# The recurrence pieces' work is queued behind the product of the preceding feed-forward block

## The chip, the cores and the metric

The kernel runs on one core of a Trainium2 chip. A core has TensorE (PE: matrix products, whose weight loads, PEld, run beside them), VectorE (DVE), ScalarE (ACT), GpSimd (POOL) and SyncE (SP), which here issues nearly all DMAs. Each engine takes its instructions in the order of its own queue and waits where an input isn't there or a buffer isn't free. The metric is the device time of one execution in microseconds: 883.58 us before, the median of 3 runs (882.69 to 884.54).

## What is computed

An mLSTM recurrence (4 batches, 8 heads, 768 tokens, head size 40) gives a [3072, 320] activation, and two gated feed-forward blocks follow, all in float32:

```
m' = max(f + m, i);  C = exp(f + m - m')*C + exp(i - m')*v k^T;  n likewise with k
y  = sigmoid(o) * (C q) / max(|n.q|, 1)                        # recurrence
x2 = (sigmoid(x @ w_gate) * (x @ w_val)) @ w_out               # block 1, d_ff 1536
out = (h * clip(h + 3, 0, 6) / 6) @ w_out2,  h = x2 @ w_in     # block 2, d_ff 2048
```

## The kernel before

The tokens are cut into 6 chunks of 128 tokens per batch, 512 columns for the matrix products. Float32 operands are split into a high and a low part, so that a product is three matmuls. A first stage, up to about 480 us, does the recurrence and block 1, interleaved; a second stage does block 2. The change touches the first stage alone.

Its loop (L858) runs over steps i = (chunk c, hidden block f, columns ts). A step is `m1_h` (L575): two groups of eight matmuls into the PSUM banks `mm` (three banks), the gate on ScalarE (L580, a sigmoid of the first bank), the product on VectorE (L581, gate times the second bank), and `split_g`, the high part on ScalarE (L567, gh) and the low part on VectorE (L568, gl). `m1_out` then multiplies gh and gl of an earlier step into `acc`. Most steps are 512 columns wide; the first 8 steps of chunk 0 and the first 12 of chunk 1 are 256 wide. Steps are counted from 0 here; step 44 is the 45th run of the loop.

The recurrence of chunk c, batch b, a set (c, b), is cut in three pieces, and as a rule one piece is issued per step, ahead of the step's `m1_h` (L863 to L871), about a chunk before block 1 needs its result:

- `att0` (L412): scores on TensorE (L363) into the two `att` banks; on VectorE two scans that turn a tile of decay factors, `dec`, into decays (L389), the values times the input gate and the decay (L354, vi and vd; for chunk 1 eight ScalarE scalings L352 make vi), and two products L404 that weigh the scores and free the two `att` banks; on ScalarE a small copy L383.
- `att1` (L426): output matmuls (L444, L455, L470, the last into a third `mm` bank), then on VectorE the chain L487, L490, L492 to L496, L354, L504 (for two sets of chunk 1 ScalarE does the scaling, eight L352), and the state update L522 and L525, which frees the `mm` bank; on ScalarE the output gate L410 and the state copies L530.
- `att2` (L532): three transposes on TensorE (L536) into an `att` bank, and the split of x on ScalarE (L541) and VectorE (L542), which frees the bank.

`dec` has two buffers. The load of the set two ahead is issued when `att1` of a set is issued (L873 to L877) and waits on SyncE for the buffer. In between `work` (L656) prepares weights: L101 (ScalarE), L119, L122 (VectorE) unpack one, L151 to L174 split one for block 1, and L632 (four times), L634 and L635 combine one for block 2.

The order of each engine's queue is not the order of the code. A list scheduler builds the queues from the traced instructions by its own costs. `tc.issue_after(ins)` sets an edge from `ins` to each instruction of its block on the same engine, so that none of them comes ahead of `ins` in the queue; on other engines it does nothing. Before, `later_chunks`, the pieces of chunk 0 and the weight work have such edges; the pieces of chunks 1 to 5 have none (L869: `opened if cp == 0 else ()`).

Of the kernel before, what the change touches and what calls it, by code (L numbers as in the profile page):

```python
# [14 lines left out]
ALU = mybir.AluOpType  # L15
# [17 lines left out]
def mlstm_then_two_gated_ffn(  # L33
# [11 lines left out]
    nc = tc.nc  # L45
# [12 lines left out]
    def ps_mm():  # L58
        return mm_ps.tile([P, 512], F32, tag="mm", name="mm")
# [132 lines left out]
    def x_tiles(key):  # L192
        x = xpool.tile([P, 2, 3, T], F32R, tag="x", name="x")
        XH[key], XL[key] = x[:, 0], x[:, 1]
# [5 lines left out]
    def att_tiles(c, b):  # L200
        if c == 0 and b > 1:
            t = slot_f32(2 * NP * L).rearrange("p (a n l) -> p a n l", a=2, l=L)
            v = slot_f32(3 * DM).rearrange("p (a n) -> p a n", a=3)
            d = slot_f32(H * L).rearrange("p (h l) -> p h l", l=L)
        else:
            t = ap.tile([P, 2, NP, L], F32, tag="qk", name="qk")
            v = ap.tile([P, 3, DM], F32, tag="vko", name="vko")
            d = ap.tile([P, H, L], F32, tag="dec", name="dec")
        at[c, b] = {"qk": t, "vko": v, "dec": d}

    def qk_load(c, b):
        nc.sync.dma_start(out=at[c, b]["qk"], in_=qkT[c, b])

    def vko_load(c, b):
        nc.sync.dma_start(out=at[c, b]["vko"], in_=vko[c, b])

    def att_load(c, b):
        att_tiles(c, b)
        qk_load(c, b)
        vko_load(c, b)  # L220

    def dec_load(c, b):
        nc.sync.dma_start(
            out=at[c, b]["dec"].rearrange("p h l -> p (h l)"),
            in_=fz_dram[c, b * H : (b + 1) * H, :]
            .rearrange("h l -> (h l)")
            .rearrange("(o n) -> o n", o=1)
            .to_broadcast([P, H * L]),
        )
# [4 lines left out]
    g = g_sb[:, :S].rearrange("p (c l) -> p c l", l=L)  # L234
# [56 lines left out]
    def later_chunks():  # L291
# [43 lines left out]
        out=sel, in_=ident[:BH, :BH].rearrange("p (n two) -> p n two", two=2),  # L335
# [4 lines left out]
        out=odd[:, :, 0], in_=ident[:BH, :BH].rearrange("p (n two) -> p two n", two=2),  # L340
# [4 lines left out]
        out=par.rearrange("p (two n) -> p two n", two=2), in_=odd.to_broadcast([BH, 2, 64])  # L345
# [186 lines left out]
    def att2(c, b, ps):  # L532
        yo = at.pop((c, b))["yo"]
        x_ps = ps()
        for k in range(3):
            nc.tensor.transpose(  # L536
                out=x_ps[:, k * P : (k + 1) * P], in_=yo[:, k * P : (k + 1) * P], identity=ident
            )
        x_v = x_ps[:, : 3 * P].rearrange("p (k t) -> p k t", k=3)
        xs = slice(b * L, (b + 1) * L)  # L540
        hi = nc.scalar.copy(out=XH[1, c][:, :, xs], in_=x_v)  # L541
        lo = nc.vector.tensor_tensor(  # L542
            out=XL[1, c][:, :, xs], in0=x_v, in1=XH[1, c].bitcast(F32)[:, :, xs], op=ALU.subtract
        )
        return hi.ins, lo.ins

    def h_pair(w, x, banks, ts=slice(0, T)):

        xh, xl = XH[x][:, :, ts], XL[x][:, :, ts]
        for j in range(2):  # L550


            tail = w[:, j, 256:384]
            nc.tensor.matmul(out=banks[j], lhsT=tail, rhs=xl[:, 2, :], start=True, stop=False)  # L554
            for k in range(2):
                hi = w[:, j, k * P : (k + 1) * P]
                lo = w[:, j, 384 + k * P : 384 + (k + 1) * P]
                nc.tensor.matmul(out=banks[j], lhsT=hi, rhs=xh[:, k, :], start=False, stop=False)  # L558
                nc.tensor.matmul(out=banks[j], lhsT=hi, rhs=xl[:, k, :], start=False, stop=False)  # L559
                nc.tensor.matmul(out=banks[j], lhsT=lo, rhs=xh[:, k, :], start=False, stop=False)  # L560
            nc.tensor.matmul(out=banks[j], lhsT=tail, rhs=xh[:, 2, :], start=False, stop=True)  # L561

    def split_g(g):
        n = g.shape[-1]
        gh = gpool.tile([P, T], F32R, tag="gh", name="gh", bufs=3)[:, :n]
        gl = gpool.tile([P, T], F32R, tag="gl", name="gl", bufs=3)[:, :n]
        nc.scalar.copy(out=gh, in_=g)  # L567
        nc.vector.tensor_tensor(out=gl, in0=g, in1=gh.bitcast(F32), op=ALU.subtract)  # L568
        return gh, gl
# [5 lines left out]
    def m1_h(c, f, ts):  # L575
        n = ts.stop - ts.start
        banks = [ps_mm()[:, :n], ps_mm()[:, :n]]
        h_pair(slots["in", f], (1, c), banks, ts)
        g = gpool.tile([P, T], F32, tag="g", name="g")[:, :n]
        gate = nc.scalar.activation(out=g, in_=banks[0], func=AF.Sigmoid).ins  # L580
        nc.vector.tensor_tensor(out=g, in0=g, in1=banks[1], op=ALU.mult)  # L581
        gs[c, f, ts.start] = split_g(g)
        return gate

    def m1_out(c, f, ts):
        if f == 0 and ts.start == 0:
# [69 lines left out]
    def work(count, limit):  # L656

        for _ in range(count):
            if len(jobs) > n_jobs - limit:
                src, use, key = jobs.pop()  # L660
                use(key, to_f32(fetched.pop(0) if fetched else fetch(src)))

    def load_out2(n):
        x = xpool.tile([P, 640], F32, tag="x2", name="w2f")
        nc.sync.dma_start(out=x, in_=wo2_dram[n])
        split_out2(("out2", n), x)
# [27 lines left out]
    with tc.manual_schedule():  # L694
# [52 lines left out]
        for b in range(2):  # L747
            opened = att2(0, b, any_ps)
# [38 lines left out]
    def x_load(pair):  # L787


        b = {}  # L790
        for k in range(2):
            for j in range(2):
                src = x2_dram[2 * pair + j]
                t = b[k, j] = late.tile([P, 640], F32, tag="c", name="xr", bufs=7)
                nc.sync.dma_start(out=t[:, 0:T], in_=src[:, k, :])
                u = late.tile([P, 2, P], F32, tag="xt", name="xu", bufs=3)
                tails = src[:, 2, :].rearrange("(two k r) (q t) -> k q r two t", two=2, k=2, q=4)[k]
                for q in range(4):
                    nc.sync.dma_start(out=u[32 * q : 32 * q + 32], in_=tails[q])
                nc.vector.tensor_tensor(out=t[:, T:], in0=u[:, 0], in1=u[:, 1], op=ALU.add)  # L800
        return x_combine(pair, b)
# [49 lines left out]
    def outputs_but(n):  # L851
        while len(before) > n:
            step = before.pop(0)
            m1_out(*step)
            if step[1] == F1 - 1:
                m1_end(step[0])

    for i, (c, f, ts) in enumerate(steps):  # L858
        if i == halves[0] - 1:
            for b in range(2):  # L860
                att_load(1, b)
                dec_load(1, b)
        for _ in range(quota[i]):  # L863
            if pieces:
                cp, b, piece = pieces.pop(0)
                if cp > 0 and b == 0 and piece == 0:
                    x_tiles((1, cp))
                with ExitStack() as queued:
                    for ins in opened if cp == 0 else ():  # L869
                        queued.enter_context(tc.issue_after(ins))  # L870
                    (att0, att1, att2)[piece](cp, b, ps_att)  # L871
                nxt = divmod(cp * B + b + 2, B)
                if cp > 0 and piece == 1 and nxt[0] < NC:  # L873
                    att_tiles(*nxt)
                    dec_load(*nxt)
                    qk_load(*nxt)
                    vko_load(*nxt)  # L877
        gate = m1_h(c, f, ts)
        outputs_but(2 if i < n_two else 1)
        before.append((c, f, ts))  # L880
        if c == 0:
            work(1 if i < 2 * halves[0] else 2, n_w1)
        elif c < NC - 1:

            with tc.issue_after(gate):
                work(c > 1 and f % 2 == 0, n_jobs)
        elif f == 0:
            assert not jobs and not pieces
            early_sb.close()
            late = ctx.enter_context(tc.tile_pool(name="late", bufs=1, reuse_waits="tile"))  # L890
            x_parts = x_load(0)
            load_group(0)
        else:
            if f > 1 and f - 2 < F2 // 2:
                load_out2(f - 2)
            next(x_parts, None)
# [187 lines left out]
```

## Time and profile before

| | |
|---|---|
| median of 3 runs | 883.58 us (882.69 to 884.54) |
| profiled execution | 884.24 us, span 882.4 us |
| mean granted TensorE clock | 0.986 of full speed |
| busy over the span | PE 842.0 us (95%), DVE 568.2 (64%), ACT 397.7 (45%) |
| chain that ended last | PE 78%, DVE 12%, DMA 7% (all of it the load of `dec`) |

Busy shares are means over stages with different limits, so they are read by stretches. The idle time of an instruction is put down to what ended it: "[2.77 <-DVE x L542]" says that the engine stood for 2.77 us before this instruction, and that L542 on VectorE released it. A granted clock of 0.50 is TensorE at 1.2 in place of 2.4 GHz. In the order of a queue the scan L389 is listed as SCALAR_TENSOR_TENSOR, in the trace as TENSOR_TENSOR_SCAN.

### The profile page before, as it was taken

What the parts mean: (1) busy time and instruction counts of PE and PEld (TensorE: products, weight loads), DVE (VectorE), ACT (ScalarE), POOL (GpSimd) and SP (SyncE); (2) the same over time, 40 slices, a digit from 0 to 9 for tenths busy, and PEclk for the clock granted to TensorE, in tenths of its full rate; (3) what the DMA queues carried; (4) which work ended last, traced back from release to release, by engine and by line L of the source; (5) the groups of instructions that cost most, each with busy time, mean ns of one, the idle gap of its engine ahead of it and who ended that gap; (6) DMA issues with size and microseconds to landing.
All of it is one profiled execution on the core that took longest, in us unless ns stands there. A gap on an engine that the chain in (4) does not pass through costs nothing.

```text
span 882.4 us, 17342 instructions
## 1 busy us (share of the span) xinstructions
PE 842.0 (95%) x7109; PEld 719.2 (82%) x7109; DVE 568.2 (64%) x1040; ACT 397.7 (45%) x807; POOL 2.5 (0%) x8
## 2 busy tenths in 40 slices
PE   6599899999999899999899999999999999999998
PEld 6498688888777777777678888888998889988898
DVE  8899965675577657765754553566846668466553
ACT  3687633322323343333322443555645556365552
POOL 1000000000000000000000000000000000000000
PEclk9999999999999999999999999999999999999999
DMA  9636623332555645564541652546635467344400
GB/s 357 231 116 230 222 71 107 116 97 71 169 174 179 207 138 208 178 207 131 180 119 54 183 138 75 180 146 198 208 97 188 145 199 216 102 157 146 145 30 30
DMA packets 69135, 135.64 MB, mean 154 GB/s; under 512 B 20672, under 2 KB 43136, under 8 KB 65984
## 3 DMA queue, kind: packets, MB, share of 16 engines
q1 hardware_dynamic: 69008, 134.44, 47.3%
q8 instruction: 56, 0.92, 0.4%
q14 instruction: 23, 0.19, 0.1%
q10 hardware_dynamic: 48, 0.10, 0.0%
HBM read 109.38 MB, written 25.13 MB: 152 GB/s over the span
## 4 chain that ended last, share of the span: by engine, by line
PE 78%; DVE 12%; DMA 7%; issue 2%; ACT 1%; SPq 0%; DVEq 0%; ACTq 0%
PE mm L910 9%; PE acc L596 8%; DMA dec<-fz_dram 7%; PE mm L558 6%; PE mm L559 6%; PE mm L560 6%; PE att L910 5%; PE acc L910 4%; PE mm L554 4%; DVE dec L389 3%; PE mm L561 3%; PE acc L606 3%; PE mm L947 2%; PE acc L947 2%; PE mm L948 2%; PE mm L949 2%
## 5 line engine op out<-in xcount | busy, mean ns | idle before, releaser
L567 ACT CAST gh<-g 128x512 fp32r<-128x512 f32 (+1 forms) x130 | 76.4, 588 | 160.4 <-DVE g L581 120.3
L558 PE MATMUL mm<-x,w 128*128 128x512 f32 (+1 forms) x328 | 123.5, 376 | 0.0
L559 PE MATMUL mm<-x,w 128*128 128x512 f32 (+1 forms) x328 | 123.1, 375 | 0.0
L560 PE MATMUL mm<-x,w 128*128 128x512 f32 (+1 forms) x328 | 122.4, 373 | 0.0
L568 DVE TENSOR_TENSOR gl<-g,gh 128x512 fp32r<-128x512 f32 (+1 forms) x130 | 84.2, 647 | 57.2 <-ACT gh L567 56.8
L596 PE MATMUL acc<-gh,w 128*128 128x512 f32 (+1 forms) x328 | 104.9, 365 | 0.0
L910 PE MATMUL mm<-X,wg 128*128 128x512 f32 x336 | 85.3, 395 | 0.0
L389 DVE TENSOR_TENSOR_SCAN dec<-dec,ident 128x512 f32<-128x512 f32 x40 | 48.0, 1216 | 53.9 <-DMA dec<-fz_dram 53.9
L581 DVE TENSOR_TENSOR g<-g,mm 128x512 f32<-128x512 f32 (+1 forms) x82 | 50.5, 616 | 47.1 <-PE mm L561 46.8
L580 ACT ACTIVATE g<-mm 128x512 f32<-128x512 f32 (+1 forms) x82 | 44.7, 545 | 76.7 <-PE mm L561 76.4
L559 PEld LDWEIGHTS mm<-x,w 128*128 128x128 f32 x328 | 64.3, 196 | 11.2
L560 PEld LDWEIGHTS mm<-x,w 128*128 128x128 f32 x328 | 64.2, 196 | 11.3
L910 PEld LDWEIGHTS mm<-X,wg 128*128 128x128 f32 x336 | 62.0, 188 | 13.5 <-DVE c L921 0.3
L558 PEld LDWEIGHTS mm<-x,w 128*128 128x128 f32 x328 | 64.5, 197 | 9.0
L554 PE MATMUL mm<-x,w 128*128 128x512 f32 (+1 forms) x164 | 68.5, 418 | 3.3 <-DVE cst L525 2.9
L596 PEld LDWEIGHTS acc<-gh,w 128*128 128x128 f32 x328 | 60.8, 190 | 10.6
L561 PE MATMUL mm<-x,w 128*128 128x512 f32 (+1 forms) x164 | 60.7, 370 | 0.0
L596 PE MATMUL acc<-gl,w 128*128 128x512 f32 (+1 forms) x164 | 60.0, 366 | 0.0
L925 ACT ACTIVATE gb<-c,half 128x512 f32<-128x512 f32 x48 | 34.5, 724 | 49.0 <-DVE c L921 49.0
L568 DVE TENSOR_TENSOR gl<-gb,gh 128x512 fp32r<-128x512 f32 x48 | 33.1, 690 | 32.3 <-ACT gh L567 32.3
L910 PE MATMUL att<-X,wg 128*128 128x512 f32 x168 | 46.8, 398 | 0.1
L567 ACT CAST gh<-gb 128x512 fp32r<-128x512 f32 x48 | 29.5, 621 | 37.9 <-PE att L948 37.9
(185 smaller groups left out, 1695.6 us busy)
## 6 DMA issues: line engine op xcount, KB each, us to landing
wg<-ws_dram SPq DMA_DIRECT2D x24, 1104.0 KB, 5.6
raw<-in_w SPq DMA_DIRECT2D x20, 640.0 KB, 5.1
qk<-in_qkT SPq DMA_DIRECT2D x22, 512.0 KB, 4.5
wg<-wt_dram SPq DMA_DIRECT2D x48, 224.0 KB, 6.2
vko<-in_vko SPq DMA_DIRECT2D x22, 480.0 KB, 6.6
dec<-fz_dram SPq DMA_DIRECT2D x20, 512.0 KB, 5.1
raw<-in_wo SPq DMA_DIRECT2D x14, 640.0 KB, 3.9
X<-xt_dram SPq DMA_DIRECT2D x84, 64.0 KB, 3.1
```

The costliest lines, as they stand in the source:

```text
L389: nc.vector.tensor_tensor_scan(out=x, data0=a["factors"][n] if "factors" in a else x, data1=ident4.rearrange("p h l -> p (h l)"), initial= ...
L554: nc.tensor.matmul(out=banks[j], lhsT=tail, rhs=xl[:, 2, :], start=True, stop=False)
L558: nc.tensor.matmul(out=banks[j], lhsT=hi, rhs=xh[:, k, :], start=False, stop=False)
L559: nc.tensor.matmul(out=banks[j], lhsT=hi, rhs=xl[:, k, :], start=False, stop=False)
L560: nc.tensor.matmul(out=banks[j], lhsT=lo, rhs=xh[:, k, :], start=False, stop=False)
L561: nc.tensor.matmul(out=banks[j], lhsT=tail, rhs=xh[:, 2, :], start=False, stop=True)
L567: nc.scalar.copy(out=gh, in_=g)
L568: nc.vector.tensor_tensor(out=gl, in0=g, in1=gh.bitcast(F32), op=ALU.subtract)
L580: gate = nc.scalar.activation(out=g, in_=banks[0], func=AF.Sigmoid).ins
L581: nc.vector.tensor_tensor(out=g, in0=g, in1=banks[1], op=ALU.mult)
L596: nc.tensor.matmul(out=a[m], lhsT=lhsT, rhs=rhs, start=st and lhsT is hi and rhs is gh, stop=en and lhsT is lo, skip_group_check=True,)
L910: nc.tensor.matmul(out=ps, lhsT=w[a][s], rhs=x[:, b, :], start=first and i == 0, stop=i == 3, skip_group_check=True,)
```

## The change

`m1_h` returns two instructions, the gate L580 (ScalarE) and the product L581 (VectorE), where it returned the gate alone. The pieces of chunks 1 to 5 are issued with edges to both, those of the step before, since the pieces of a step are issued ahead of its own `m1_h`. The weight work keeps its edge to the gate alone.

```diff
--- before.py
+++ after.py
@@ -578,9 +578,9 @@
         h_pair(slots["in", f], (1, c), banks, ts)
         g = gpool.tile([P, T], F32, tag="g", name="g")[:, :n]
         gate = nc.scalar.activation(out=g, in_=banks[0], func=AF.Sigmoid).ins
-        nc.vector.tensor_tensor(out=g, in0=g, in1=banks[1], op=ALU.mult)
+        mult = nc.vector.tensor_tensor(out=g, in0=g, in1=banks[1], op=ALU.mult).ins
         gs[c, f, ts.start] = split_g(g)
-        return gate
+        return gate, mult
 
     def m1_out(c, f, ts):
         if f == 0 and ts.start == 0:
@@ -866,7 +866,7 @@
                 if cp > 0 and b == 0 and piece == 0:
                     x_tiles((1, cp))
                 with ExitStack() as queued:
-                    for ins in opened if cp == 0 else ():
+                    for ins in opened if cp == 0 else gate:
                         queued.enter_context(tc.issue_after(ins))
                     (att0, att1, att2)[piece](cp, b, ps_att)
                 nxt = divmod(cp * B + b + 2, B)
@@ -882,7 +882,7 @@
             work(1 if i < 2 * halves[0] else 2, n_w1)
         elif c < NC - 1:
 
-            with tc.issue_after(gate):
+            with tc.issue_after(gate[0]):
                 work(c > 1 and f % 2 == 0, n_jobs)
         elif f == 0:
             assert not jobs and not pieces
```

So no VectorE instruction of a piece of chunks 1 to 5 stands ahead of the preceding step's product, and no ScalarE instruction ahead of its gate. The number and kind of the computing instructions stay, SyncE's and GpSimd's queues are the same row by row, and TensorE's queue differs in the first twelve steps only. On VectorE and ScalarE much moves; three places show it. Numbers behind a name tell tiles apart.

VectorE, steps 44 and 45 (g_3773 and g_3820 are their products; dec_3520 and dec_3751 are the decay tiles of two successive sets). Before:

```order
L581 TENSOR_TENSOR g_3773<-g_3773,mm_3756 128x512
L122 SCALAR_TENSOR_TENSOR bits_3792<-raw_3788,bits_3792 128x640
L568 TENSOR_TENSOR gl_3777<-g_3773,gh_3776 128x512
L389 SCALAR_TENSOR_TENSOR dec_3751<-dec_3751,ident4_81 128x512 x2
L542 TENSOR_TENSOR x_2888<-att_3796,x_2888 128x3x128
L354 TENSOR_TENSOR vi_4043<-vko_3750,iT_83 128x8x40
L354 TENSOR_TENSOR vd_4048<-vi_4043,dec_3751 128x328
L581 TENSOR_TENSOR g_3820<-g_3820,mm_3803 128x512
L568 TENSOR_TENSOR gl_3824<-g_3820,gh_3823 128x512
L404 TENSOR_TENSOR dec_3520<-att_3836,dec_3520 128x4x128
L404 TENSOR_TENSOR dec_3520<-att_3837,dec_3520 128x4x128
```

With the change, the same two steps:

```order
L581 TENSOR_TENSOR g_3773<-g_3773,mm_3756 128x512
L122 SCALAR_TENSOR_TENSOR bits_3792<-raw_3788,bits_3792 128x640
L568 TENSOR_TENSOR gl_3777<-g_3773,gh_3776 128x512
L542 TENSOR_TENSOR x_2888<-att_3796,x_2888 128x3x128
L581 TENSOR_TENSOR g_3820<-g_3820,mm_3803 128x512
L389 SCALAR_TENSOR_TENSOR dec_3520<-dec_3520,ident4_81 128x512 x2
L568 TENSOR_TENSOR gl_3824<-g_3820,gh_3823 128x512
L354 TENSOR_TENSOR vi_3846<-vko_3519,iT_83 128x8x40
L354 TENSOR_TENSOR vd_3851<-vi_3846,dec_3520 128x328
L404 TENSOR_TENSOR dec_3520<-att_3836,dec_3520 128x4x128
L404 TENSOR_TENSOR dec_3520<-att_3837,dec_3520 128x4x128
```

and step 47:

```order
L581 TENSOR_TENSOR g_4013<-g_4013,mm_3996 128x512
L389 SCALAR_TENSOR_TENSOR dec_3751<-dec_3751,ident4_81 128x512 x2
L568 TENSOR_TENSOR gl_4017<-g_4013,gh_4016 128x512
L354 TENSOR_TENSOR vi_4043<-vko_3750,iT_83 128x8x40
L354 TENSOR_TENSOR vd_4048<-vi_4043,dec_3751 128x328
L404 TENSOR_TENSOR dec_3751<-att_4033,dec_3751 128x4x128
L404 TENSOR_TENSOR dec_3751<-att_4034,dec_3751 128x4x128
```

The scans of dec_3751 go from step 44 to step 47, the step in which that tile is weighed; those of dec_3520, which were three steps earlier too, now stand in step 45. L542 follows L568 directly. In the same way the scans of nearly all sets move three to four steps back in the queue, and so do vi and vd, the copy L383, and L522.

VectorE, steps 5 and 6 (g_1024 is step 6's product; dec_732 and vd_1075 belong to the second set of chunk 1, den_934 and yo_949 to its first). Before:

```order
L496 RECIPROCAL den_934<-den_934 128x8
L119 TENSOR_SCALAR bits_999<-u_997 128x640
L568 TENSOR_TENSOR gl_984<-g_980,gh_983 128x256
L122 SCALAR_TENSOR_TENSOR bits_999<-raw_995,bits_999 128x640
L389 SCALAR_TENSOR_TENSOR dec_732<-dec_732,ident4_81 128x512 x2
L504 TENSOR_TENSOR yo_949<-y_935,vko_725 128x320
L171 TENSOR_TENSOR w_1002<-bits_999,w_1002 128x2x64
L174 TENSOR_TENSOR w_1002<-bits_999,w_1002 128x2x256
L581 TENSOR_TENSOR g_1024<-g_1024,mm_1007 128x256
L119 TENSOR_SCALAR bits_1043<-u_1041 128x640
L354 TENSOR_TENSOR vd_1075<-vi_1063,dec_732 128x328
```

With the change:

```order
L496 RECIPROCAL den_934<-den_934 128x8
L119 TENSOR_SCALAR bits_999<-u_997 128x640
L568 TENSOR_TENSOR gl_984<-g_980,gh_983 128x256
L122 SCALAR_TENSOR_TENSOR bits_999<-raw_995,bits_999 128x640
L504 TENSOR_TENSOR yo_949<-y_935,vko_725 128x320
L171 TENSOR_TENSOR w_1002<-bits_999,w_1002 128x2x64
L174 TENSOR_TENSOR w_1002<-bits_999,w_1002 128x2x256
L581 TENSOR_TENSOR g_1024<-g_1024,mm_1007 128x256
L119 TENSOR_SCALAR bits_1043<-u_1041 128x640
L389 SCALAR_TENSOR_TENSOR dec_732<-dec_732,ident4_81 128x512
L568 TENSOR_TENSOR gl_1028<-g_1024,gh_1027 128x256
L122 SCALAR_TENSOR_TENSOR bits_1043<-raw_1039,bits_1043 128x640
```

The two scans leave the place between L122 and L504 and go behind the product of step 6; vd and the weighing L404 go on to step 7.

ScalarE, steps 2 and 3 (vi_803 and vi_1063 are the values of the first two sets of chunk 1). Before:

```order
L580 ACTIVATE g_706<-mm_688 128x256
L352 ACTIVATE vi_803<-vko_725,iT_83 128x40
L101 ACTIVATE u_780<-raw_778 128x640
L352 ACTIVATE vi_803<-vko_725,iT_83 128x40 x4
L165 CAST w_720<-bits_717 128x2x320
L567 CAST gh_709<-g_706 128x256
L580 ACTIVATE g_760<-mm_742 128x256
L383 COPY vi_803<-iT_83 128x8
L101 ACTIVATE u_854<-raw_852 128x640
```

With the change:

```order
L580 ACTIVATE g_706<-mm_688 128x256
L101 ACTIVATE u_780<-raw_778 128x640
L165 CAST w_720<-bits_717 128x2x320
L567 CAST gh_709<-g_706 128x256
L580 ACTIVATE g_760<-mm_742 128x256
L352 ACTIVATE vi_803<-vko_725,iT_83 128x40 x6
L511 COPY yo_682<-yo_682 128x64
L352 ACTIVATE vi_803<-vko_725,iT_83 128x40 x2
L541 CAST x_122<-att_736 128x3x128
L383 COPY vi_803<-iT_83 128x8
L567 CAST gh_763<-g_760 128x256
```

The eight scalings of vi_803, which began in step 1, stand in one run behind the gate of step 3 and ahead of the cast of that step, gh_763.

## Rows read from the trace of the kernel before

**Rows 1.** Busy time by stretch (stretch, length, PE, PEld, DVE, ACT, POOL, clock).
```profile
40.00:101.00 61.00, 57.67 (x732) 51.11 (x722) 58.52 (x129) 47.07 (x132) 0.00 (x0) 1.00 0.59 201
240.00:480.00 240.00, 228.03 (x2273) 181.33 (x2272) 156.44 (x292) 78.47 (x152) 0.00 (x0) 0.96 0.50 162
```

**Rows 2.** What TensorE waited for, 101 to 480 us (total, times, longest).
```profile
PE att L363 <- DVE x L542: 5.9, 3, 2.8
PE att L455 <- DVE x L542: 5.5, 2, 3.5
PE att L536 <- DVE dec L404: 4.8, 3, 2.4
```

**Rows 3.** What VectorE waited for in the same stretch.
```profile
DVE dec L389 <- DMA dec<-fz_dram: 53.9, 15, 8.8
```

**Rows 4.** Timeline of three engines around 304 us (start, duration, instruction).
```profile
299.09 0.38 SPq L223 DMA_DIRECT2D dec<-fz_dram  x1
304.18 0.48 PE L363 MATMUL att<-qk 40*128 40x128 f32 x2
304.60 2.34 DVE L389 TENSOR_TENSOR_SCAN dec<-dec,ident 128x512 f32<-128x512 f32 x2 [4.57 <-DMA dec<-fz_dram]
306.86 0.53 DVE L542 TENSOR_TENSOR x<-att,x 128x384 fp32r<-128x384 f32 x1
307.44 1.62 PE L363 MATMUL att<-qk 40*128 40x128 f32 x14 [2.77 <-DVE x L542]
```

**Rows 5.** Span and mean granted clock, and two slices (columns as in rows 1).
```profile
core 0: 882.4 us, clock 0.986
...
152.00:156.00 4.00, 4.00 (x20) 3.78 (x19) 1.50 (x3) 0.38 (x1) 0.00 (x0) 0.50 0.00 0
180.00:184.00 4.00, 3.01 (x17) 2.41 (x16) 3.44 (x7) 0.73 (x3) 0.00 (x0) 1.00 0.00 0
```

**Rows 6.** TensorE's timeline from the end of one step's products on.
```profile
102.92 0.39 PE L596 MATMUL acc<-gh,w 128*128 128x512 f32 x1
...
111.57 0.49 PE L536 MATMUL att<-ident,yo 128*128 128x128 f32 x3
```

**Rows 7.** VectorE's instructions by shape, 40 to 480 us (busy, mean ns, idle before).
```profile
L389 DVE TENSOR_TENSOR_SCAN dec<-dec,ident 128x512 f32<-128x512 f32 x40 | 48.0, 1216 | 53.9 <-DMA dec<-fz_dram 53.9
L568 DVE TENSOR_TENSOR gl<-g,gh 128x512 fp32r<-128x512 f32 x50 | 34.5, 689 | 22.4 <-ACT gh L567 22.4
L581 DVE TENSOR_TENSOR g<-g,mm 128x512 f32<-128x512 f32 x50 | 34.0, 679 | 16.1 <-PE mm L561 15.7 <-ACT yo L511 0.3
L404 DVE TENSOR_TENSOR dec<-att,dec 128x512 f32<-128x512 f32 x40 | 25.5, 679 | 1.6 <-PE att L363 1.6
L122 DVE SCALAR_TENSOR_TENSOR bits<-raw,bits 128x640 int32<-128x640 int32 x31 | 25.4, 819 | 0.4
L635 DVE TENSOR_TENSOR bits<-bits,ws 128x1120 fp32r<-128x1120 f32 x8 | 10.6, 1326 | 2.4 <-ACT ws L634 2.4
L354 DVE TENSOR_TENSOR vd<-vi,dec 128x328 f32<-128x328 f32 x16 | 8.0, 497 | 0.4
L632 DVE TENSOR_TENSOR bits<-bits 128x160 f32<-128x160 f32 x32 | 9.1, 316 | 0.2
```

**Rows 8.** Timeline of VectorE and TensorE in half-width steps.
```profile
178.06 1.23 DVE L389 TENSOR_TENSOR_SCAN dec<-dec,ident 128x512 f32<-128x512 f32 x1 [2.05 <-DMA dec<-fz_dram]
...
181.37 0.55 PE L536 MATMUL att<-ident,yo 128*128 128x128 f32 x3 [0.99 <-DVE dec L404]
```

**Rows 9.** The saturated beginning: TensorE, VectorE, and ScalarE's scalings by shape.
```profile
100.94 0.50 PE L554 MATMUL mm<-x,w 128*128 128x512 f32 x1 [2.94 <-DVE cst L525]
...
69.06 2.33 DVE L389 TENSOR_TENSOR_SCAN dec<-dec,ident 128x512 f32<-128x512 f32 x2
71.31 0.46 DVE L504 TENSOR_TENSOR yo<-y,vko 128x320 f32<-128x320 f32 x1
...
L352 ACT ACTIVATE vi<-vko,iT 128x40 f32<-128x40 f32 x24 | 6.3, 319 | 0.4 <-PE att L455 0.4
```

## The prediction

> **What bounds the kernel now.** I read the table of stretches first, because a share over the whole span hides where TensorE stands. [Rows 1] has two stretches of the first stage, with TensorE, its weight loads, VectorE, ScalarE and GpSimd in that order. From 40 to 101 us VectorE is busy 58.52 of 61 us: there VectorE sets the pace. From 240 to 480 us TensorE is busy 228.03 of 240 us, VectorE only 156.44, and the granted clock is 0.96. There TensorE is the bound, and what it loses is waiting and clock.
>
> Next, who TensorE waits for. [Rows 2]: in 101 to 480 us it waits 5.9 us for L542, 5.5 us for L542 again and 4.8 us for L404, all on VectorE; 16.2 us. The two take 0.53 and 0.68 us themselves [rows 4, 7], so the next view is what held VectorE: the scans of L389 waited 53.9 us in 15 places for the load of the decay rows [rows 3].
>
> [Rows 4] shows one place. The load of a decay tile is issued at 299.09. VectorE reaches the two scans of that tile, stands still for 4.57 us, and starts them at 304.60, when the load has landed. TensorE has begun the scores at 304.18 and sticks after two matmuls: the other bank is still read by L542, which stands behind the scans. It goes on at 307.44, after 2.77 us. The scanned tile (dec_3751 in the order) isn't weighed before step 47; VectorE blocked for something that nobody needed for three more steps.
>
> The third view is the clock. The mean granted clock is 0.986 over 882.4 us, so 12.4 us are lost; [rows 5] has a slice at 0.50, that is TensorE at 1.2 in place of 2.4 GHz, right behind one of these waits. A little of it falls where TensorE idles anyway; I take 12.0.
>
> What a page says of this: the Trainium skill ("TensorE: Matmul & The Clock Gate", section "What's actually happening") puts the ramp penalty at under 1% of a typical span. That would be at most 8.8 us here and the sum 3.2 us higher; the trace has 12.4 us, 1.4%, so the trace decides.
>
> **The change part by part.** No arithmetic is added or removed; the instructions of the recurrence pieces move behind the product L581 (VectorE) and the gate L580 (ScalarE) of the step before. No DMA moves: SyncE's queue keeps its order, and so the loads their place.
>
> *The stall on the load.* In the new order the scans of a tile stand in the step in which the tile is weighed (dec_3751 in step 47 in the first extract), three steps after the place at which they waited. Three steps are more than the 8.65 us of [rows 6], and the load landed 5.5 us after its issue [rows 4], so it is there when they come. So the 53.9 us of VectorE's waiting go, and with them the 16.2 us of TensorE. Bounds: 0 if something else on VectorE is late at each of the eight places, 16.2 if nothing is. What is late next is the weighing, now in one chain behind the product. From the end of a step's products to the transposes that need the freed bank TensorE has from 102.92 to 111.57, 8.65 us of other work [rows 6]. VectorE's chain is 0.68 (L581) + 2 x 1.216 (scans) + 0.69 (L568) + 2 x 0.50 (L354 twice) + 0.68 (first weigh) = 5.5 us, by [rows 7]. It fits with 3 us to spare. In the half-width steps around 181 the margin is nil: scans that needn't wait start 2.05 us sooner, the two L354 that now come ahead of the weigh take 1.0, and the wait there was 0.99 [rows 8]. I take the whole 16.2.
>
> *The clock.* If the waits go, so do the slow stretches behind them: 12.0 us. Bounds 0 and 12.4. The wait of 0.99 us at 181 lies in a slice at 1.00 [rows 5, 8], so short leftovers may stay without a price on the clock.
>
> *New: steps with a weight combination.* Three scan steps (38, 50 and 62) also hold L122, four L632 and L635. With those the chain is 5.5 + 0.82 + 4 x 0.32 + 1.33 = 8.9 us, and some 0.2 until it starts: 9.1 against 8.65, so 0.45 us each, 1.3 us in all. Bounds 0 (the means overlap a little at their ends) and 3 x 2.77 = 8.3, were each as bad as the wait of [rows 4].
>
> *New: the saturated beginning.* From 40 to 101 us there is no slack on VectorE, and TensorE at last waits 2.94 us for L525 at 100.94 [rows 9]. What changes ahead of L525: one scan of the third set of chunk 1 goes behind it, -1.2. The second extract: without the two scans L504 directly follows L122 in step 5 and waits for ScalarE, which scales eight heads first. Before, the scans filled this time, from 69.06 to 71.31. The new idle is between 0 and 2.25 us; ScalarE needs 8 x 0.319 = 2.55 for eight heads [rows 9], partly beside L119, L568 and L122, so I take 1.5. The third extract: the eight scalings of chunk 1's first values, until now put into gaps of ScalarE over steps 1 to 3, now stand between the gate of step 3 and the cast that VectorE's L568 waits for. That is 0 to 2.55 us; as VectorE is busy 96% there, nearly all of it comes through, and I take 2.4. Together +2.7 us. Bounds: -2.9 (the wait at 100.94 vanishes) and 2.25 + 2.55 = +4.8 (both waits in full, and the scan that goes behind gives nothing).
>
> *ScalarE elsewhere.* The copies L383 and the output gates that stood too early and waited move too. ScalarE is busy 78.47 of 240 us [rows 1]; nothing there is priced.
>
> Sum, against the profiled execution's own 884.24 us (span 882.4 and 1.8 around it; the median of the runs is 883.58, 0.07% lower): 884.24 - 16.2 - 12.0 + 1.3 + 2.7 = **860.0 us**, 2.7% less.
>
> **The rivals.**
>
> *A: short waits remain and keep the clock low.* The three combination steps stall for longer, 0.9 us, twice my 0.45, and each is followed by a slow stretch of 1.5 us, an estimate: the 12.0 us shared among the eight waits of [rows 2]. And the beginning costs its upper 4.8. 884.24 - 28.2 + 3 x (0.9 + 1.5) + 4.8 = 868.0. For it: the chain has no margin in these steps. Against: the slice at 1.00 with the wait of 0.99 us [rows 5, 8].
>
> *B: the beginning costs nothing.* VectorE is busy with the same work there and has one scan less ahead of L525; if the shorter queue also ends the wait at 100.94, 884.24 - 28.2 - 2.9 + 1.3 = 854.4.
>
> *C: no change.* TensorE is busy 228.03 of 240 us [rows 1] and its own matmuls would bound it, with VectorE's waiting free. Then 884. The Trainium skill ("Perfetto Trace Analysis", section "Identifying the Most-Contended Engine") says to optimize the engine of the highest occupancy first, and VectorE isn't that after 101 us. Against: [rows 2] and [rows 4] name VectorE as what TensorE waits for, and the same section goes on to the gaps of the busy engine.
>
> *D: slower.* The weighing becomes late at every set. One mechanism: if VectorE carries a backlog so that L581 starts over 3 us after its products are done, the scans behind it finish after TensorE has reached the transposes, which delays the next products and so on. It decides from 5.5 + 3.1 > 8.65 us. Were each of the 18 sets after the first two to wait 2.0 us, the mean of the eight waits in [rows 2], and the slow stretches to stay, 884.24 - 16.2 + 18 x 2.0 + 2.7 = 906.7. For it: until 101 us VectorE does run behind. Against: after 101 us it is busy 65% and has 53.9 us of waiting to give back.
>
> **How the numbers follow.** Forecast 0.70, A 0.13, B 0.08, C 0.04, D 0.05. The forecast's own uncertainty (the beginning from 0 to 4.8, the combination steps from 0 to 3) is about 856 to 864. For 8 in 10 the range has to take in B and most of A: 853 to 871. A measurement of this kernel tells some 0.2%, 1.8 us, from no change. Faster: forecast, A and B, 0.91; same: C, 0.04; slower: D, 0.05.
>
> **What the profile after would show.** Right: the wait of L389 for the load falls from 53.9 to a few us; TensorE's waits for L542 and L404 after 101 us fall from 16.2 to under 3; the granted clock over the span is 0.995 or more; the stage's end is some 24 us earlier and the later stage as long as before. At the beginning L504 of step 5 waits for ScalarE, and TensorE gets past L525's wait 2 to 3 us later than 100.94. Wrong: L389 still waits for loads in its new place, or TensorE waits for L404 at most sets (D), or waits go and the clock still dips (A).

## The result, and the profile after

The kernel after takes **858.99 us** (median of four runs, 858.3 to 860.77); the kernel before, beside it, 883.13 (879.35 to 884.54). The ratio is 0.9736, 95% interval 0.9702 to 0.977. The forecast was 860.0. Ratios, here and below, are of fast executions; one execution of run 4, 913.7 us at a granted clock of 0.856, is slow and is not in its ratio and range.

The stretches of [rows 1] again, in the kernel after, in the same columns:

```profile
40.00:101.00 61.00, 57.72 (x733) 50.76 (x723) 56.74 (x124) 45.23 (x122) 0.00 (x0) 1.00 0.59 199
240.00:480.00 240.00, 240.00 (x2363) 192.16 (x2362) 167.60 (x313) 87.94 (x172) 0.00 (x0) 1.00 0.55 174
```

From 240 to 480 us TensorE is busy all the time at a clock of 1.00; before it was busy 228.03 us at 0.96. It gets through 2363 matmuls in these 240 us, in place of 2273.

What TensorE waited for from 101 to 480 us, the answer to [rows 2]:

```profile
PE mm L554 <- DVE cst L525: 3.1, 1, 3.1
PE att L536 <- DVE dec L404: 0.4, 1, 0.4
```

The 16.2 us for L542 and L404 have become 0.4. The other row is the wait at the end of the saturated beginning, which [rows 9] shows as 2.94 us. In VectorE's list of waits L389 no longer appears at all, where [rows 3] has 53.9 us.

The same set of decay rows as in [rows 4], in the timeline after:

```profile
287.59 0.38 SPq L223 DMA_DIRECT2D dec<-fz_dram  x1
...
295.21 1.16 PE L363 MATMUL att<-qk 40*128 40x128 f32 x16
...
307.79 0.69 DVE L581 TENSOR_TENSOR g<-g,mm 128x512 f32<-128x512 f32 x1
...
308.39 2.34 DVE L389 TENSOR_TENSOR_SCAN dec<-dec,ident 128x512 f32<-128x512 f32 x2
...
312.35 1.29 DVE L404 TENSOR_TENSOR dec<-att,dec 128x512 f32<-128x512 f32 x2
```

The load is issued at 287.59 and VectorE comes to the two scans at 308.39, 20.8 us later, right behind the product. They start without a wait. The scores that [rows 4] shows torn into 2 and 14 belong to the step in which these scans stood before, three steps earlier; after, they run at 295.21 as one group of 16 matmuls.

Span and mean granted clock:

```profile
core 0: 856.5 us, clock 0.998
```

The one slow place that is left from 40 to 480 us, in the columns of [rows 1]:

```profile
102.00:104.00 2.00, 1.56 (x4) 1.27 (x5) 1.97 (x6) 1.74 (x9) 0.00 (x0) 0.58 0.65 266
104.00:106.00 2.00, 2.00 (x7) 1.57 (x6) 1.26 (x3) 1.95 (x7) 0.00 (x0) 0.56 0.32 74
```

By slices of 2 us the kernel before lost 11.9 us to the clock between 101 and 480 us: 3.4 once and 1.7 five times. The kernel after loses (0.42 + 0.44) x 2 = 1.7, behind the wait for L525. The whole stretch, before and after, shows the same more coarsely (a mean clock of 0.97 over 379 us is some 11 us):

```profile
101.00:480.00 379.00, 362.70 (x3913) 296.69 (x3914) 243.78 (x473) 128.15 (x274) 0.00 (x0) 0.97 0.44 142
```
```profile
101.00:480.00 379.00, 377.12 (x4025) 309.26 (x4026) 262.47 (x502) 141.08 (x307) 0.00 (x0) 1.00 0.49 155
```

The sum of what the rows show: waits 0.4 - 16.2 = -15.8, clock 1.7 - 11.9 = -10.2, a later end of the beginning (102.44 for 100.94) +1.5; together -24.5. The span fell by 882.4 - 856.5 = 25.9, all of it ahead of block 2's products: the first matmul of L910 starts at 520.9, before at 546.8, and from there to the end both take 335.6 us. 1.4 us have no row of their own; with the two traces laid side by side, matmul by matmul, they are spread over some six places of 0.1 to 0.35 us.

### The profile page after: what moved, and what is told of

Same layout as the page of the kernel before. It is cut to its first block, busy times and chain, and to the rows that moved or that the text cites. A ratio compares the mean times of both kernels' runs of the same rounds, so it can differ in the third digit from the quotient of the medians.

```text
span 856.5 us, 17379 instructions
## 1 busy us (share of the span) xinstructions
PE 830.4 (97%) x7109; PEld 710.5 (83%) x7109; DVE 571.4 (67%) x1040; ACT 398.1 (46%) x807; POOL 2.5 (0%) x8
## 4 chain that ended last, share of the span: by engine, by line
PE 91%; DVE 5%; ACT 1%; issue 1%; DMA 1%; DVEq 0%; ACTq 0%; SPq 0%
PE acc L596 11%; PE mm L910 9%; PE mm L558 8%; PE mm L559 8%; PE mm L560 8%; PE mm L554 5%; PE att L910 5%; PE acc L910 5%; PE acc L606 4%; PE mm L561 4%; PE att L363 3%; PE mm L947 2%; PE acc L947 2%; PE mm L948 2%; PE mm L949 2%; PE acc L948 2%
## 5 line engine op out<-in xcount | busy, mean ns | idle before, releaser
L558 PE MATMUL mm<-x,w 128*128 128x512 f32 (+1 forms) x328 | 121.2, 370 | 0.0
L559 PE MATMUL mm<-x,w 128*128 128x512 f32 (+1 forms) x328 | 121.2, 369 | 0.0
L560 PE MATMUL mm<-x,w 128*128 128x512 f32 (+1 forms) x328 | 121.0, 369 | 0.0
L568 DVE TENSOR_TENSOR gl<-g,gh 128x512 fp32r<-128x512 f32 (+1 forms) x130 | 84.0, 646 | 54.4 <-ACT gh L567 54.1
L581 DVE TENSOR_TENSOR g<-g,mm 128x512 f32<-128x512 f32 (+1 forms) x82 | 50.7, 618 | 69.5 <-PE mm L561 69.2
L580 ACT ACTIVATE g<-mm 128x512 f32<-128x512 f32 (+1 forms) x82 | 44.7, 545 | 100.4 <-PE mm L561 100.2
L910 PE MATMUL mm<-X,wg 128*128 128x512 f32 x336 | 85.1, 394 | 0.0
L910 PEld LDWEIGHTS mm<-X,wg 128*128 128x128 f32 x336 | 62.1, 188 | 13.3 <-DVE c L921 0.3
L560 PEld LDWEIGHTS mm<-x,w 128*128 128x128 f32 x328 | 62.6, 191 | 10.8
L559 PEld LDWEIGHTS mm<-x,w 128*128 128x128 f32 x328 | 62.5, 191 | 10.8
L554 PE MATMUL mm<-x,w 128*128 128x512 f32 (+1 forms) x164 | 66.9, 408 | 3.9 <-DVE cst L525 3.1
L558 PEld LDWEIGHTS mm<-x,w 128*128 128x128 f32 x328 | 62.6, 191 | 8.9
L561 PE MATMUL mm<-x,w 128*128 128x512 f32 (+1 forms) x164 | 60.2, 367 | 0.0
L568 DVE TENSOR_TENSOR gl<-gb,gh 128x512 fp32r<-128x512 f32 x48 | 33.1, 690 | 32.2 <-ACT gh L567 32.2
L389 DVE TENSOR_TENSOR_SCAN dec<-dec,ident 128x512 f32<-128x512 f32 x40 | 47.2, 1211 | 0.0
L910 PE MATMUL att<-X,wg 128*128 128x512 f32 x168 | 46.8, 398 | 0.2 <-DVE g L926 0.2
```

What stands on the lines that cost most here:

```text
L389: nc.vector.tensor_tensor_scan(out=x, data0=a["factors"][n] if "factors" in a else x, data1=ident4.rearrange("p h l -> p (h l)"), initial= ...
L581: mult = nc.vector.tensor_tensor(out=g, in0=g, in1=banks[1], op=ALU.mult).ins
L910: nc.tensor.matmul(out=ps, lhsT=w[a][s], rhs=x[:, b, :], start=first and i == 0, stop=i == 3, skip_group_check=True,)
```

## Experiments

The theory: a scan that stands in VectorE's queue where its load hasn't landed blocks work that TensorE needs. The rivals: the place in the queue costs whatever the load takes; the two edges share the gain; other work than the scans is in the way. Ratios are to the kernel before on the same chip. The edits are shown short: lines that only set up an empty list, or hand the product on, are not printed. Where an edit adds lines, L542 reads L545 in its rows, L404 stays, and so on.

**1. The order of before, a shorter load.**

```diff
-out=at[c, b]["dec"].rearrange("p h l -> p (h l)"),
+out=at[c, b]["dec"].rearrange("p h l -> p (h l)")[: 8 if c > 0 else P],
-.to_broadcast([P, H * L]),
+.to_broadcast([8 if c > 0 else P, H * L]),
-data0=a["factors"][n] if "factors" in a else x,
+data0=a["factors"][n] if "factors" in a else x if c == 0 else ident4.rearrange("p h l -> p (h l)"),
```

> The kernel before with its own order of instructions on TensorE, VectorE and ScalarE; from chunk 1 on the load of a decay tile writes 8 of 128 partitions (32 KB in place of 512 KB) and the two scans of L389 read a constant, while they still wait for that load. Left out are the other 15/16 of the load and the use of the decay rows in chunks 1 to 5. Theory (the early scans stand in VectorE's queue ahead of work that TensorE needs, and wait there for the load): the 64 KB loads of the page land in 3.1 us, the 512 KB loads in 4.9 us, so a scan waits some 2 to 2.5 us less at each of its 15 places; L389 waits 18 to 28 us in place of 53.9, TensorE's waits for L542 and L404 after 101 us fall from 16.2 to under 4 us, the slow clock behind them goes, and the time is 856 to 864 us with the order of before. Rival (the place in the queue is what costs, whatever the load takes): 880 to 884 us.

856.37 us (855.6 to 858.12), ratio 0.972 [0.9695, 0.9744]. Waits of VectorE and TensorE, 101 to 480 us:

```profile
DVE dec L389 <- DMA dec<-fz_dram: 25.7, 13, 5.7
...
PE att L455 <- DVE x L542: 0.6, 1, 0.6
PE att L363 <- DVE x L542: 0.5, 1, 0.5
PE att L536 <- DVE dec L404: 0.2, 1, 0.2
```

With every instruction of the three engines where it was, and the scans as long as before (1.22 us), a shorter wait alone brings the whole gain. The rival falls. The run also moves less data in all, so that other loads may land sooner; but in the kernel before TensorE waits for no load from 40 to 480 us, and VectorE, beside L389, 1.2 us. And VectorE still waits 25.7 us in 13 places, which leave TensorE 1.3 us of waits for L542 and L404: most of the shorter waits fit into its slack, those of before did not.

**2 and 3. One edge at a time.** The edge to the product alone, then the edge to the gate alone:

```diff
-for ins in opened if cp == 0 else gate:
+for ins in opened if cp == 0 else gate[1:]:     # run 2
+for ins in opened if cp == 0 else gate[:1]:     # run 3
```

> The kernel after with the edge to the product L581 alone: the VectorE work of the pieces goes behind it, the ScalarE work is ordered freely again. Theory (all of the gain is VectorE's): 857 to 860 us, L389 waits for no load, and the eight L352 scalings of chunk 1 go back into gaps of ScalarE, so L525's wait of TensorE near 102 us starts to end earlier by 0 to 1.5 us. Rival (the two edges share the gain): 866 to 876 us.

858.39 us (857.65 to 859.3), ratio 0.974 [0.9717, 0.9764]: all of the gain. The end of L525's wait came no earlier, against the expectation; it is at 102.76.

> The kernel after with the edge to the gate L580 alone: ScalarE's work of the pieces goes behind it, VectorE's scans stand three steps ahead of their use as in the kernel before. Theory: VectorE still waits 45 to 60 us at L389 for the load; 881 to 887 us. Rival (the two edges share the gain): 866 to 876 us.

873.88 us (871.38 to 875.03), ratio 0.9912 [0.9884, 0.9939]. The expectation of 881 to 887 was wrong; the number is the rival's. What VectorE waited for at the scans, and TensorE for L525, 40 to 480 us:

```profile
DVE dec L389 <- DMA dec<-fz_dram: 43.4, 13, 7.8
...
PE mm L554 <- DVE cst L525: 1.6, 1, 1.6
```

VectorE still waits for the load, and TensorE's waits for L542 and L404 are 12.1 us in place of 16.2; that for L525 is 1.6 in place of 2.9. The order of that kernel shows what the expectation left out: the edge on ScalarE also moved VectorE's L354 (vd<-vi,dec), which needs a value that ScalarE writes, from behind the scans to some steps later. Run 9 does that alone.

**9. L354 of the last decay alone behind the product.**

```diff
-if c < NC - 1:
-    values_end(c, b, c == 0)
+with ExitStack() as queued:
+    for ins in last_gate if c > 0 else ():   # the product of the step before
+        queued.enter_context(tc.issue_after(ins))
+    if c < NC - 1:
+        values_end(c, b, c == 0)
```

> The kernel before with only the scaling by the last decay (L354, vd<-vi,dec, 0.50 us) of chunks 1 to 4 moved behind the product of the step before its step; the scans stay three steps early, TensorE's, ScalarE's and SyncE's orders are those of before. Theory (in the run with the ScalarE edge alone it was this instruction, gone from behind the waiting scans, that brought most of its 8 us: each wait of TensorE 0.5 us shorter, and some of the slow stretches gone): 874 to 879 us, TensorE's waits for L542 and L404 after 101 us at 11 to 14 us in place of 16.2. Rival (ScalarE's own moved work brought it): 880 to 883 us.

878.45 us (872.34 to 882.82), ratio 0.9943 [0.9907, 0.998]. Its waits, 101 to 480 us:

```profile
DVE dec L389 <- DMA dec<-fz_dram: 47.3, 14, 7.6
...
PE att L539 <- DVE dec L404: 5.1, 3, 2.4
PE att L363 <- DVE x L545: 4.8, 3, 2.1
PE att L458 <- DVE x L545: 4.2, 2, 2.3
```

The edge on these 16 instructions of 0.50 us takes TensorE's waits from 16.2 to 14.1 us, just over the 14 expected, and the time down by some 5 us (2 to 8 by the interval), where run 3 has 8. The intervals of runs 3 and 9 overlap. Part of what lies between them is L525's wait, 2.9 us here as in the kernel before and 1.6 in run 3, which this instruction doesn't explain; the rest stays open.

**5. The scans alone behind the product.**

```diff
-for n in range(2):
-    decays(c, b, n)
+with ExitStack() as queued:
+    for ins in last_gate if c > 0 else ():   # the product of the step before
+        queued.enter_context(tc.issue_after(ins))
+    for n in range(2):
+        decays(c, b, n)
```

> The kernel before with one thing moved: the two scans of L389 of chunks 1 to 5 stand behind the product L581 of the step before their step; all other work of the pieces has no edge, on VectorE as on ScalarE. Theory (the scans that wait for the load are the whole cause): L389 waits under 5 us for loads, TensorE's waits for L542 and L404 after 101 us are under 3 us, and the time is 856 to 861 us, all of the gain of the kernel after. Rival (the other VectorE work, as L354, stands in the way too, since the ScalarE edge alone, which moved L354, brought 8 us): 864 to 876 us.

860.8 us (858.87 to 861.3), ratio 0.978 [0.9764, 0.9797]. Waits, 101 to 480 us:

```profile
DVE vi L354 <- DMA vko<-in_vko: 33.2, 7, 8.0
...
PE att L458 <- DVE x L545: 2.1, 2, 1.1
PE att L447 <- DVE dec L404: 1.1, 1, 1.1
PE att L539 <- DVE dec L404: 1.0, 2, 0.6
```

The scans are most of it, not all (a ratio of 0.978, where both edges reach 0.9708 to 0.9736): TensorE's waits are 4.2 us, over the 3 I had allowed. The next early instruction, L354 (vi<-vko,iT), now waits 33.2 us in their place, for the load behind the decay rows. That these 33.2 us cost so little, without 2.4 us of scans behind each wait, I argue and have not shown by itself.

**8. Before with a third buffer.**

```diff
-d = ap.tile([P, H, L], F32, tag="dec", name="dec")
+d = ap.tile([P, H, L], F32, tag="dec", name="dec", bufs=3)
+# vd, y and yo: bufs=1
```

> The kernel before without any edge, with a third buffer for the decay tiles (and one buffer in place of two for the tiles vd, y and yo), so that a load can be issued one set earlier. The scans then stand six to nine products ahead of their weighing in place of three. Theory (what costs is a scan that stands in the queue where the load has not yet landed; an order that puts it as early as the load is due keeps the wait): L389 waits 25 to 55 us again and the time is 872 to 886 us. Rival (the scans wait because two buffers bring the load too late, and one more buffer cures it): L389 waits under 8 us, 856 to 862 us.

875.66 us (871.35 to 876.18), ratio 0.9935 [0.9914, 0.9957]. Waits of VectorE from 40 to 480 us, then one place in the timeline:

```profile
DVE vi L354 <- DMA vko<-in_vko: 29.8, 6, 6.3
...
DVE dec L389 <- DMA dec<-fz_dram: 20.3, 10, 3.7
```
```profile
298.53 0.49 DVE L354 TENSOR_TENSOR vi<-vko,iT 128x320 f32<-128x320 f32 x1 [5.56 <-DMA vko<-in_vko]
...
298.94 1.22 DVE L389 TENSOR_TENSOR_SCAN dec<-dec,ident 128x512 f32<-128x512 f32 x1
...
300.52 1.21 DVE L389 TENSOR_TENSOR_SCAN dec<-dec,ident 128x512 f32<-128x512 f32 x1
...
300.66 1.48 PE L363 MATMUL att<-qk 40*128 40x128 f32 x14 [3.35 <-DVE x L542]
```

The load is issued earlier (at 291.59 for the set that is weighed at 343.33; before, at 324.02 for the same set, weighed at 351.24), and that brings some 6 us and no cure: the scans move up with it, most of them six and more products ahead of their use, and other early work waits for the next load. VectorE's list of waits has none for the tiles that went from two buffers to one. A third buffer with the order of before held fast was not run. L389's own wait came out under the 25 us I had expected; with L354's it is 50.1 us, near the 53.9 of before. The time is within the theory's range, though this profile is that of the fastest run.

**4. The edges two steps earlier.**

```diff
-for ins in opened if cp == 0 else gate:
+for ins in opened if cp == 0 else gates[-3]:
-gate = m1_h(c, f, ts)
+gate = m1_h(c, f, ts); gates.append(gate)
```

> The kernel after with its edges to the gate and the product of two steps earlier: the scans of L389 stand two products ahead of their weighing (after: none, before: mostly three). Theory (only the wait for the load costs; the load is issued right behind the recurrence products four steps ahead of the weighing and lands 5.5 us later, less than one step): L389 waits under 5 us in all, and the time is that of the kernel after or 1 to 3 us less, 855 to 860 us. Rival (nearness to the product before the use is what helps): a third of the way back per product, 868 to 878 us.

855.5 us (854.35 to 855.61), ratio 0.9707 [0.9673, 0.9741]. Waits from 40 to 480 us:

```profile
DVE dec L389 <- DMA dec<-fz_dram: 5.6, 2, 3.4
...
PE mm L554 <- ACT g L580: 1.5, 1, 1.5
PE mm L554 <- DVE cst L525: 1.4, 1, 1.4
```

Two products ahead of their use the scans find their data in all but two places, and TensorE waits for nothing else. What counts is whether the load has landed; nearness to the use brings nothing, and by TensorE's waits it costs a little in the beginning, where this kernel has 2.9 us of them and the kernel after some 4.7. The ratios (0.9707 here, 0.9736 and 0.9708 for the kernel after) don't tell the two apart.

**6 and 7. L525 ahead of two weight splits**, on the kernel after (6) and on that of run 4 (7). The splitting of step 10, first used at step 14, is issued behind step 11's L525:

```diff
+if late_work and states:                     # states: the L525 of the piece just issued
+    with tc.issue_after(states.pop()):
+        work(*late_work.pop())
 gate = m1_h(c, f, ts)
...
-work(1 if i < 2 * halves[0] else 2, n_w1)
+work(*late_work.pop()) if late_work else None; late_work.append((2, n_w1)) if i >= 10 else work(1 if i < 2 * halves[0] else 2, n_w1)
```

> The kernel after with the weight splitting of step 10 issued behind L525 of the piece of step 11. Theory (at 99.4 us TensorE waits 3.07 us for L525 only because two weight splits stand ahead of it on VectorE, and those are first used three steps later): the wait at 102.44 falls below 1 us, the slow clock of 1.7 us behind it goes, and the time is 858.99 - 3.1 - 1.7 = 854.2 us, 853 to 856. Rival (VectorE is busy 93% until 101 us, so the split work shifted back makes TensorE wait elsewhere by as much): 858 to 861 us.

854.2 us (853.76 to 855.31), ratio 0.9705 [0.969, 0.972]. In the timeline, L525 and TensorE's one wait from 95 to 111 us:

```profile
96.07 0.33 DVE L525 TENSOR_TENSOR cst<-cst,mm 104x164 f32<-104x164 f32 x1
...
110.25 0.55 PE L536 MATMUL att<-ident,yo 128*128 128x128 f32 x3 [1.88 <-DVE dec L404]
```

L525 runs at 96.07 in place of 102.07, and its wait, the one of 0.85 us for the gate ahead of it, and the slow clock are gone. 1.88 us come back at 110.25, where the weighing is late behind the delayed splits: part of the rival is true. That the time met the expected 854.2 is partly luck, as neither the 0.85 nor the 1.88 was in its sum.

> The kernel with the edges two steps earlier (855.5 us), and with the weight splitting of step 10 behind L525 as well. Theory: its two waits of TensorE near 97 and 101 us, 1.50 for the gate and 1.42 for L525, lose the second and perhaps the first: 852.5 to 854.5 us. Rival (VectorE saturated, the wait only moves): 855 to 857 us.

**852.56 us** (852.12 to 852.95), ratio 0.9685 [0.967, 0.9699]. From 40 to 480 us TensorE has one wait:

```profile
PE att L536 <- DVE dec L404: 0.4, 1, 0.4
```

**10. After once more.**

> The kernel after unchanged, on the chip on which its relatives are timed: 857 to 861 us, ratio to before 0.972 to 0.977. It is there so that the version with the edges two steps earlier and L525 ahead of the splitting (852.56 us, ratio 0.9685) has a kernel after of the same ratio to stand against.

858.25 us (857.12 to 858.53), ratio 0.9708 [0.9669, 0.9748]; the time is as expected, the ratio just under 0.972. No run of after is below 857.12 and none of run 7 above 852.95: the version of run 7 beats both kernels, before by 3.2% and after by some 0.7%.

## Why the prediction was right, and where it was not

**The stall on the load** was the cause, as forecast. The waits of TensorE went from 16.2 to 0.4 us [rows 2], with L389's from 53.9 to none [rows 3]. Run 1 shows that the length of the wait for the load is what costs; runs 2 and 5 that VectorE's edge, and in it mostly the scans, carries the gain. The 0.4 us that stay are a wait of the transposes for L404 at 164.76, in a half-width step, where the forecast saw no margin. What the forecast left out is L354: behind the scans it prolongs the block (run 9), and without them it waits itself (run 5).

**The clock**: 12.0 forecast, 10.2 measured. The six slow places behind the waits vanished, but one of 1.7 us came at 102.44, behind the wait for L525. The forecast gave that wait no price on the clock; the kernel before has none behind it:

```profile
102.00:104.00 2.00, 2.00 (x10) 1.66 (x9) 1.88 (x5) 1.97 (x7) 0.00 (x0) 1.00 0.39 161
```

The Trainium skill ("TensorE: Matmul & The Clock Gate", section "What's actually happening") says of the warm-up that, for modeling, the ramp penalty is under 1% of a typical span. The slow stretches here come behind waits in the middle of the kernel; they took 11.9 us of 882.4, 1.3%, before, and 0.2% after, so the figure covers only the second.

**The combination steps**: +1.3 forecast, 0 measured, the lower bound. This term of the sum failed: no wait of TensorE is left in any of the three steps. One of those steps after:

```profile
328.03 0.68 DVE L581 TENSOR_TENSOR g<-g,mm 128x512 f32<-128x512 f32 x1
...
328.63 0.82 DVE L122 SCALAR_TENSOR_TENSOR bits<-raw,bits 128x640 int32<-128x640 int32 x1
...
330.24 1.22 DVE L389 TENSOR_TENSOR_SCAN dec<-dec,ident 128x512 f32<-128x512 f32 x1
...
331.38 0.77 DVE L632 TENSOR_TENSOR bits<-bits 128x160 f32<-128x160 f32 x3
...
334.12 1.32 DVE L635 TENSOR_TENSOR bits<-bits,ws 128x1120 fp32r<-128x1120 f32 x1
...
335.35 1.28 DVE L404 TENSOR_TENSOR dec<-att,dec 128x512 f32<-128x512 f32 x2
...
336.33 0.49 PE L536 MATMUL att<-ident,yo 128*128 128x128 f32 x3
```

From L581's start to the end of the first weigh it is 335.35 + 1.28 / 2 - 328.03 = 8.0 us, where I added the means to 8.9 and 0.2 for the start. Neighbours on VectorE start 0.05 to 0.1 us before the one ahead has ended (the scan of 1.22 us is followed after 1.14), and the first of the two weighs frees the bank. The transposes at 336.33 come 0.3 us later: the margin is there, and thin.

**The saturated beginning**: +2.7 forecast, +1.5 measured, and made of other parts. These are its waits of TensorE that are new or longer, L504 on VectorE, and step 3's cast on ScalarE with L568 behind it on VectorE:

```profile
62.41 0.50 PE L470 MATMUL mm<-vd,vko 128*32 128x41 f32 x32 [0.22 <-DVE vd L354]
...
79.35 0.52 PE L536 MATMUL att<-ident,yo 128*128 128x128 f32 x3 [0.58 <-DVE dec L404]
...
97.27 0.50 PE L554 MATMUL mm<-x,w 128*128 128x512 f32 x1 [0.85 <-ACT g L580]
...
102.44 0.79 PE L554 MATMUL mm<-x,w 128*128 128x512 f32 x1 [3.07 <-DVE cst L525]
...
70.61 0.49 DVE L504 TENSOR_TENSOR yo<-y,vko 128x320 f32<-128x320 f32 x1 [0.60 <-ACT y L352]
...
56.82 0.41 ACT L567 CAST gh<-g 128x256 fp32r<-128x256 f32 x1
...
57.59 0.41 DVE L568 TENSOR_TENSOR gl<-g,gh 128x256 fp32r<-128x256 f32 x1
```

0.22 + 0.58, and 0.46 and 0.13 more than before in the two waits for L580 and L525, are 1.4 of the 1.5 us; TensorE's order differs in these steps too, so this is a sum of waits and no more. L504 does wait for ScalarE, 0.60 us where I took 1.5. The 2.4 us for the eight scalings behind the gate are nothing: the cast behind them ends at 57.23, and VectorE, busy until then with other work, comes to L568 at 57.59 without a wait. With the product's edge alone the scalings stand in gaps again (run 2), and TensorE gets past L525's wait no sooner, at 102.76. TensorE was 1.5 us later there, where I had said 2 to 3.

The forecast charged 1.3 us too much for the combination steps and 1.2 for the beginning, and took 1.8 us too much gain from the clock and 0.4 from the waits; these nearly cancel, and what is left to the profiled 858.3 us are the 1.4 us without a row. That 860.0 came so close to 858.99 is partly luck. **Rivals**: A's short waits did not come in the combination steps; B was too low by the beginning; C (TensorE's own matmuls as the bound) is refuted by the result and by run 1, D by the 0.4 us.

## What to carry to other kernels

Where an engine in order waits for a transfer, look at what stands behind it in its queue and who needs that, and when the result of the waiting instruction is used; moved to where its data had landed, it cost nothing here. A load issued earlier, into another buffer, brought only some 6 us while the order followed the load up (run 8). Two steps of lead were as good as none here and left the beginning freer: an edge need be no stronger than the landing asks for.

## What the runs showed of the hardware

**The mean clock is not a price.** The kernel after in run 10 and in its first profile, same stretch, columns as in [rows 1]:

```profile
20.00:40.00 20.00, 9.63 (x182) 7.55 (x186) 17.57 (x40) 10.43 (x31) 0.00 (x0) 0.55 0.66 228
```
```profile
20.00:40.00 20.00, 10.06 (x182) 7.95 (x185) 17.57 (x40) 10.40 (x31) 0.00 (x0) 1.00 0.65 223
```

At 0.55 and at 1.00 TensorE does the same 182 matmuls, and is busy for only about half of the 20 us, since it waits for others there; the clock over the span is 0.984 against 0.998, the spans 856.7 and 856.5 us. What a slow clock costs has to be read from stretches in which TensorE has work.

**The length of a wait alone doesn't tell whether the clock falls behind it.** At about 101 us the wait of 2.94 us was followed by none in the kernel before, and by a stretch at 0.50 in run 1, where it also was 2.94; behind 1.25 us at 394.91 in the kernel before there was one, behind 1.88 us in run 6 none. The stretch in run 1, where the kernel before has 1.00 (above, under the clock):

```profile
102.00:104.00 2.00, 2.00 (x6) 1.53 (x5) 2.00 (x4) 2.00 (x10) 0.00 (x0) 0.50 0.33 105
```

What decides is open.
